# An FFT convolution with a routed expert layer behind it: where the expert work of the last pairs and the sums for their routing stand

## The chip, the core and the metric

The kernel runs on one core of one Trainium2 chip. The metric is device time in microseconds (us) for one execution. The engines are TensorE (PE; PEld is its weight loads), VectorE (DVE), ScalarE (ACT), GpSimd (POOL), and SyncE (SP), which issues most of the transfers.

## The reference

```python
Yf = rfft(x, 2 * S, axis=1) * rfft(h, 2 * S, axis=0)[None]    # x: 8 x 6336 x 128
x = irfft(Yf, 2 * S, axis=1)[:, :S]                            # a causal long convolution
scores = einsum('bsd,d->bs', x, w_gate)
out = x.copy()
for b in range(8):
    top = argpartition(-scores[b], 128)[:128]                  # 128 rows of each batch
    y = maximum(x[b, top] @ w1, 0) @ w2                        # 128 -> 1024 -> 128
    out[b, top] = x[b, top] + sigmoid(scores[b, top])[:, None] * y
```

## The kernel before

The convolution is a product of transforms over a factored length, 99 by 64. The work comes in eight **units**: a unit is a pair of batches with half of the features, so units 2p and 2p+1 make up pair p. One unit goes through four steps. `stage_a` multiplies the folded input (VectorE folds it, `fold`) by a 99-point table. `stage_b` does the 64-point transforms ("n2 visits", 13 chunks of k) and multiplies by the filter's spectrum on VectorE and GpSimd (`times`). `stage_c` goes back over 64 (64 columns s), and `stage_d` back over 99, and writes the unit out.

Before the loop, groups 0 to 15 of `stage_a` run for the filter and unit 0 (here called the start), with `fill`, a few products that nobody reads, behind every second group; then `stage_b_first`. The loop over i (**stage** i) has 32 items. Items 0 to 15 run `stage_c` of unit i, four columns each, and items 16 to 31 run `stage_d`. A `plan` puts `stage_a` of unit i+1 at items 0 to 8 and `stage_b` of unit i+1 at items 14 to 28, two chunks at a time. All instruction streams are fixed when the program is written; each engine runs its own in order.

The scores need no pass of their own: `weigh(i, c)` adds one column of the spectrum, times its gate weight, into `acc` on VectorE, 64 times per unit. These sums are emitted inside `stage_c`, ahead of column s those with n below 2s+5 in the last stage. After the sums of both units of a pair, `route(p)` goes on in small **visits**, called by `aside`: `scores`, then `pick`, an eight-way search in 11 steps (`search`: compare and count on VectorE, a small product on TensorE at line 428), then ranks, and the row numbers `iu`. Then `gather` fetches the 128 chosen rows by an indirect transfer from GpSimd's queue, for either half u of the features, and `feed` runs `expert` for both batches in visits: a transposition (line 534), two halves of the first product (line 546), and the second product (line 558), whose result goes back by two indirect transfers (line 562).

What is emitted when is set by counters that the program keeps, not by the chip: `t["pe"]` grows by 0.47 per column of `stage_c`, 0.89 per product group of `stage_d` and by the `on_pe` of the others; `t["dve"]` runs ahead of it by the `on_dve` of VectorE's work. A visit names the counter value at which the next may come (`after_dve` returns `t["dve"]` plus 0.3), and `aside` compares.

Pair 0's experts run in stage 3, pair 1's in stage 5, pair 2's in stage 7, the last one, and pair 3's behind it. What waits behind the last stage, until the last rows are written and gathered, is filled with unread products (`idle`): 9 from `route` and 5 from the closing loop.

Of the kernel before, what the change touches and what calls it, by code (L numbers as in the profile page):

```python
# [35 lines left out]
def conv_moe(ctx, tc, x, h, wg_d, w1, w2, fa_d, wb_d, wc_d, at_d, wgl_d, tri_d, cst_d, tw_d, fb_d, *out):  # L36
# [62 lines left out]
    ones16 = cp.tile([128, 128], BF16, name="ones16")  # L99
    upper16 = cp.tile([128, 128], BF16, name="upper16")  # L100
# [20 lines left out]
    def make_constants():  # L121
        v.tensor_copy(out=upper16, in_=upper)
# [180 lines left out]

    def stage_c(i):
# [90 lines left out]
    def pick(b0, ss, picked):  # L395
# [64 lines left out]
        for t in range(2):  # L460
            pe.matmul(pt[0:N1, 264 + 2 * t:266 + 2 * t], upper16[0:N1, 0:N1], rows[:, t], start=True, stop=t == 0)
        pe.matmul(pt[0:N1, 266:268], ones16[0:N1, 0:N1], rows[:, 0], start=False, stop=True)
# [23 lines left out]
        for b in range(2):  # L486
            iu = new([128, 1], U32, "iu", bufs=2)
            v.tensor_scalar(out=iu, in0=col[:, b:b + 1], scalar1=float(b0 * S), scalar2=None, op0=ALU.add)
            picked.append(iu)
# [5 lines left out]
    def gather(b0, picked, u, j, r):  # L495
        if u == 0:
            r.append((picked[j], new([CAP, 2, 64], F32, "xe", bufs=2)))
# [4 lines left out]
    def feed(b0, got, work):  # L502
        if b0 + 2 < B:
            yield after_act(16.0)
        while work is apart and phase[0] < NU - 1:
            yield 1
        todo = []
        for j, (iu, xt) in enumerate(got):
            todo.append(expert(b0, iu, xt, lambda shape, tag, j=j: work(shape, tag, j)))
# [10 lines left out]
    def shared(shape, tag, j):  # L520
        return new(shape, F32, tag)
# [8 lines left out]
    def expert(b0, iu, xt, work):  # L530
# [24 lines left out]
        yield 1  # L555
        py = ps()
        for f in range(NF):
            pe.matmul(py[:, 0:D], hm[f], w2s[:, f], start=(f == 0), stop=(f == NF - 1))  # L558
        on_pe(1.9)
# [15 lines left out]
    def route(p):  # L575
        b0 = 2 * p
        while weighed[0] < 2 * p + 2 or (fed and b0 + 2 < B):
            yield
# [4 lines left out]
        got = []  # L583
        for u in range(2):
            while (u or b0 + 2 < B) and (phase[0] < 2 * p + 2 or (b0 + 2 < B and place[0] < 4)):
                yield
            for j in range(2):
                gather(b0, picked, u, j, got)
                if b0 + 2 < B and place[0] > 10:
# [13 lines left out]
    fed = []  # L603
# [10 lines left out]
    with tc.manual_schedule():  # L614
# [16 lines left out]
        wide = acc.rearrange("p t b c k -> p (t b c k)")[:, 0:512]  # L631
        v.memset(wide[:, 128:512], 1.0)
# [5 lines left out]
        for g in range(16):  # L638
# [5 lines left out]
            if g % 2:  # L644
# [12 lines left out]
        for i in range(NU):  # L657
# [11 lines left out]
            for item in range(32):  # L669
# [13 lines left out]
                if i == NU - 1 and item == 16:  # L683
                    ready[1] = 0.0
                    aside()
                    aside()
                if item in plan:
                    aside()
                    for kind, k in plan[item]:
                        if kind == "a":  # L690
# [4 lines left out]
                            elif q == 0 and g % 8 == 7:  # L695
                                fold(g + 1, v)
# [10 lines left out]
                issue(item == 31)  # L707
            for st in (cs, ds):
# [3 lines left out]
        assert not fed  # L712
        for _ in routes:
            idle(5)
# [134 lines left out]
```

## Time and profile before

| what | value |
|---|---|
| time, median of 3 runs (lowest to highest) | 895.11 us (892.11 to 895.34) |
| the profiled execution: its time, its span | 894.62 us, 892.9 us |
| mean granted TensorE clock in it | 0.995 |
| busy: PE, DVE, ACT, POOL | 866.3, 697.3, 348.0, 304.0 us |
| the chain that ended last: PE, DVE, DMA | 77%, 14%, 4% |

The span runs from the first to the last instruction; 1.7 us of the execution lie outside it. A busy PE is not a PE at its peak, since matmuls overlap and their ends are modelled.

### The profile page before, as it was taken

What the parts mean: (1) busy time and instruction counts of PE and PEld (TensorE: products, weight loads), DVE (VectorE), ACT (ScalarE), POOL (GpSimd) and SP (SyncE); (2) the same over time, 40 slices, a digit from 0 to 9 for tenths busy, and PEclk for the clock granted to TensorE, in tenths of its full rate; (3) what the DMA queues carried; (4) which work ended last, traced back from release to release, by engine and by line L of the source; (5) the groups of instructions that cost most, each with busy time, mean ns of one, the idle gap of its engine ahead of it and who ended that gap; (6) DMA issues with size and microseconds to landing.
All of it is one profiled execution on the core that took longest, in us unless ns stands there. A gap on an engine that the chain in (4) does not pass through costs nothing.

```text
span 892.9 us, 37277 instructions
## 1 busy us (share of the span) xinstructions
PE 866.3 (97%) x16656; PEld 764.3 (86%) x16656; DVE 697.3 (78%) x1608; ACT 348.0 (39%) x405; POOL 304.0 (34%) x268
## 2 busy tenths in 40 slices
PE   8899999999999999999999999999999999999996
PEld 6699898789987998889987898889987899789875
DVE  6468976568699989967499989867589987977761
ACT  4523671147311751156401671147311572125321
POOL 0058306520355006630355105640265204650102
PEclk9999999999999999999999999999999999999998
DMA  8659567846585667655376566855467535840150
GB/s 296 208 178 356 178 217 228 265 156 193 180 279 191 199 198 244 216 191 198 107 230 208 179 209 204 262 162 178 133 216 234 183 118 157 276 140 33 33 185 28
DMA packets 76379, 170.76 MB, mean 191 GB/s; under 512 B 9786, under 2 KB 26136, under 8 KB 76219
## 3 DMA queue, kind: packets, MB, share of 16 engines
q1 hardware_dynamic: 75194, 167.32, 58.4%
q8 instruction: 131, 2.15, 1.0%
q0 software_dynamic: 1024, 1.05, 0.5%
q14 instruction: 30, 0.24, 0.1%
HBM read 135.38 MB, written 32.96 MB: 189 GB/s over the span
## 4 chain that ended last, share of the span: by engine, by line
PE 77%; DVE 14%; DMA 4%; issue 3%; ACT 1%; POOL 1%; POOLq 0%; ACTq 0%; SPq 0%; DVEq 0%
PE pb L318 26%; PE pb L348 18%; PE pb L177 12%; PE pb L214 10%; PE pb L264 4%; DVE tx L223 3%; DMA ht<-hd 3%; DVE slots L223 3%; DVE cmp L419 2%; PE m L546 1%; PE m L629 1%; PE m L558 1%; PE m L377 1%; DVE num L422 1%; DVE thr L435 1%
## 5 line engine op out<-in xcount | busy, mean ns | idle before, releaser
L234 POOL TENSOR_TENSOR slots<-slots,tx 128x512 f32<-128x512 f32 (+1 forms) x182 | 232.6, 1310 | 355.7 <-DVE tx L223 342.7
L318 PE MATMUL pb<-wc,slots 64*99 64x128 f32 x4096 | 241.5, 272 | 0.9 <-POOL slots L279 0.9
L318 PEld LDWEIGHTS pb<-wc,slots 64*99 64x99 f32 x4096 | 226.8, 167 | 9.4 <-POOL slots L279 1.3
L348 PE MATMUL pb<-slots,at 99*99 99x256 f32 (+1 forms) x1040 | 231.0, 374 | 2.5 <-issue 1.1
L348 PEld LDWEIGHTS pb<-slots,at 99*99 99x99 f32 x1040 | 161.8, 163 | 58.2 <-issue 6.0
L322 ACT COPY slots<-pb 99x1024 f32<-99x1024 f32 x128 | 143.3, 1119 | 127.2 <-PE pb L318 119.7
L359 ACT COPY yt<-pb 99x1024 f32<-99x1024 f32 x63 | 63.9, 1014 | 329.8 <-PE pb L348 324.8
L214 PEld LDWEIGHTS pb<-slots 128*64 128x64 f32 x5544 | 167.9, 136 | 14.5 <-issue 12.9
L214 PE MATMUL pb<-slots 128*64 128x64 f32 x5544 | 175.8, 222 | 1.4 <-issue 1.4
L302 DVE SCALAR_TENSOR_TENSOR acc<-slots,wgl,acc 128x198 f32<-128x198 f32 x496 | 170.2, 419 | 2.7 <-POOL slots L234 2.7
L223 DVE TENSOR_TENSOR slots<-pb,ht 128x512 f32<-128x512 f32 (+1 forms) x182 | 119.5, 657 | 47.6 <-PE pb L214 36.2
L186 ACT COPY slots<-pb 128x792 f32<-128x792 f32 x138 | 114.9, 918 | 23.9 <-PE pb L177 23.9
L223 DVE TENSOR_TENSOR tx<-pb,ht 128x512 f32<-128x512 f32 (+1 forms) x182 | 118.9, 653 | 0.0
L177 PE MATMUL pb<-fa,xr 50*64 50x99 f32 x1952 | 94.4, 248 | 1.3 <-DVE tx L276 0.9
L177 PEld LDWEIGHTS pb<-fa,xr 50*64 50x64 f32 x1952 | 85.7, 133 | 10.4 <-issue 4.9
L177 PE MATMUL pb<-fa,two 50*64 50x99 f32 x1344 | 66.0, 247 | 0.2 <-issue 0.2
L562 POOL DMA_INDIRECT out<-xe,iu x16 | 16.1, 1003 | 138.7 <-DVE xe L560 123.4
L279 POOL TENSOR_TENSOR slots<-slots,tx 128x256 f32<-128x256 f32 (+1 forms) x50 | 39.4, 809 | 58.6 <-DVE tx L276 57.3
L177 PEld LDWEIGHTS pb<-fa,two 50*64 50x64 f32 x1344 | 58.8, 132 | 0.4 <-issue 0.3
L177 PE MATMUL pb<-fa,slots 50*64 50x99 f32 x1312 | 48.9, 253 | 5.5 <-issue 5.4
L177 PEld LDWEIGHTS pb<-fa,slots 50*64 50x64 f32 x1312 | 44.4, 138 | 8.8 <-issue 6.3
L166 DVE TENSOR_TENSOR xr<-xr 128x512 f32<-128x512 f32 x61 | 42.9, 703 | 2.0
(143 smaller groups left out, 596.5 us busy)
## 6 DMA issues: line engine op xcount, KB each, us to landing
slots<-tab_wb SPq DMA_DIRECT2D x86, 512.0 KB
xr<-in_x SPq DMA_DIRECT2D x61, 512.0 KB
out<-yt SPq DMA_DIRECT2D x63, 396.0 KB
ht<-hd SPq DMA_DIRECT2D x84, 256.0 KB
at<-tab_at SPq DMA_DIRECT2D x128, 153.1 KB
hd<-slots SPq DMA_DIRECT2D x12, 512.0 KB
xr<-tab_wb SPq DMA_DIRECT2D x9, 512.0 KB
slots<-in_h SPq DMA_DIRECT2D x8, 512.0 KB
```

Source lines behind the costliest of these rows:

```text
L166: eng.tensor_tensor(out=a[:, 0], in0=a[:, 0], in1=a[:, 1], op=ALU.add)
L177: pe.matmul(pt[c * 64:c * 64 + 64, b, d * N1:(d + 1) * N1], src, fa[rows, c], start=True, stop=True)
L186: act.copy(out=dst, in_=src)
L214: pe.matmul(banks[c][g * 64:g * 64 + 64, j * 64:j * 64 + 64], wt[:, j, c * 64:c * 64 + 64], y[:, g, :, k0 + j], start=True, stop=True)
L223: v.tensor_tensor(out=dst, in0=banks[c][:, 0:kn * 64].rearrange("p (k b j t) -> p k b j t", k=kn, b=2, t=2), in1=ht[t].rearrange("p k (j t ...
L234: pool.tensor_tensor(out=d3, in0=d3, in1=tx.rearrange("p k (j t) -> p k j t", t=2), op=ALU.add if c else ALU.subtract)
L279: pool.tensor_tensor(out=d3, in0=d3, in1=tx[:, c, 0:w].rearrange("p k (j t) -> p k j t", t=2), op=ALU.add if c else ALU.subtract)
L302: v.scalar_tensor_tensor(out=dst, in0=col, scalar=w, in1=dst, op0=ALU.mult, op1=ALU.add)
L318: pe.matmul(pair[0:N1, g, s % 4 * 128:s % 4 * 128 + 128], y[rows, s // 2, ri, :, s % 2], wc[rows, ri], start=(ri == 0), stop=(ri == 1))
L322: act.copy(out=z[:, s // 4], in_=pair[0:N1].rearrange("p g (j t m) -> p (g j) t m", j=2, t=2))
L348: pe.matmul(pt[0:N1, o:o + w * 128], ats[tau // 2][:, tau % 2, c], z[:, c, q:q + w], start=(c == 0), stop=(c == 1))
L359: act.copy(out=yt.rearrange("p n b q d -> p n q b d"), in_=src.rearrange("p (n q b d) -> p n q b d", n=w, q=4, b=2))
```

## The change

It does eight things. (1) In the start, `fill` comes after groups 1 and 3 alone, with 384 columns for 512. (2) In stage 6 the n2 visits of unit 7 stand at items 11 to 23 in place of 14 to 28. (3) 30 of unit 7's 64 sums are emitted at items 26 to 31 of stage 6. (4) The first two folds of the next unit go from items 6 to 8 of a stage to items 29 and 30. (5) `feed` is no longer called from `aside` but from `feeder`, at plan items; it takes both experts of a pair one step further per visit, at least 2.5 apart. If it begins by item 8 (`alone`), the two output tiles `yt` are its scratch space, and the next `route` may begin meanwhile. (6) Of pair 2's eight expert visits three stay in the last stage and five come behind it. (7) All four gathers of pair 3 come behind the last stage, batch by batch; then pair 2's five visits, 8 unread products, the closing loop's 5, and pair 3's experts in another order. (8) The last two output tiles lie in `flat` and not in the two `yt` buffers. The diff, without some declarations:

```diff
@@ stage_c
             while n < min(64, (5 if i < NU - 1 else 8) * s // 4 + 5):
-                weigh(i, n)
+                if n >= early[0]:
+                    weigh(i, n)
                 n += 1
...
-            if i == NU - 1 or (fed and s % 4 == 1):
+            if i == NU - 1:
                 aside()
@@ stage_d
-                yt = tp.tile([N1, 2, 2, 4, 64], F32, tag="y", name="yt", bufs=2)[:, 0:w]
+                if alone:
+                    yt = flat[0:N1, 8192 + n * 512:8704 + n * 512]
+                else:
+                    yt = tp.tile([128, 1024], F32, tag="y", name="yt", bufs=2)[0:N1]
@@ feed
-        if b0 + 2 < B:
-            yield after_act(16.0)
-        while work is apart and phase[0] < NU - 1:
+        last = b0 + 4 >= B
+        if not last:
+            alone[0] = place[0] <= 8
+            if alone[0]:
+                sides = [tp.tile([128, 1024], F32, tag="y", name="yt", bufs=2) for _ in got]
+            else:
+                sides = [None, two.rearrange("p a n -> p (a n)")]
+        while last and phase[0] < NU - 1:
             yield 1
...
         if b0 + 2 == B:
-            for j in (0, 1, 0, 0, 1, 0, 1, 1, 0, 1):
-                next(todo[j], None)
+            for j in (0, 0, 0, 1, 0, 1, 1, 1):
+                next(todo[j])
+        elif last:
+            for j in (0, 1):
+                next(todo[j])
+            yield after_act(2.5)
+            while place[0] < 16:
+                yield 1
+            next(todo[0])
+            while phase[0] < NU:
+                yield 1
+            for n, j in enumerate((0, 1, 1, 0, 1)):
+                while n == 3 and not gathered[0]:
+                    yield 1
+                next(todo[j])
+                yield 1
         else:
-            for g in todo:
-                for n, _ in enumerate(g):
-                    yield after_act(1.7)
-                    while work is apart and g is todo[1] and n == 2 and place[0] < 16:
-                        yield 1
+            for _ in range(4):
+                for g in todo:
+                    next(g)
+                yield after_act(2.5)
@@ route
-        while weighed[0] < 2 * p + 2 or (fed and b0 + 2 < B):
+        while weighed[0] < 2 * p + 2 or (fed and b0 + 2 < B and not alone[0]):
             yield
...
+        if b0 + 2 == B:
+            while phase[0] < NU:
+                yield
+            for j in range(2):
+                for u in range(2):
+                    gather(b0, picked, u, j, got)
+            gathered[0] = True
+            while fed:
+                ready[1] = 0.0
+                feeder()
+            idle(8)
+            yield 0
+            yield from feed(b0, got)
+            return
...
-        if b0 + 2 < B:
-            fed.append(feed(b0, got, shared if b0 + 4 < B else apart))
-        else:
-            idle(9)
-            yield 0
-            yield from feed(b0, got, apart)
+        ready[1] = after_act(16.0)
+        fed.append(feed(b0, got))
@@ aside, which no longer feeds
-        if t["pe"] >= ready[0] and (place[0] >= 16 or phase[0] >= NU - 1 or t["dve"] < t["pe"] + 1.0):
+        if t["pe"] >= ready[0] and (quiet[0] or place[0] >= 16 or phase[0] >= NU - 1 or t["dve"] < t["pe"] + 1.0):
             ready[0] = next(routes, None) or 0.0
+
+    def feeder():
         if fed and t["pe"] >= ready[1]:
             ready[1] = next(fed[0], None) or 0.0
...
@@ the start
-                pe.matmul(pt, plain[:, 0:128], wide, start=True, stop=True)
+                pe.matmul(pt[:, 0:384], plain, wide, start=True, stop=True)
...
-            if g % 2:
+            if g in (1, 3):
                 fill(1)
@@ the loop over the stages
-                for n, at_item in enumerate((14, 16, 18, 20, 23, 26, 28)):
+                for n, at_item in enumerate((14, 16, 18, 20, 23, 26, 28) if i < NU - 2 else (11, 13, 15, 17, 19, 21, 23)):
...
-                if i == NU - 1 and item == 16:
-                    ready[1] = 0.0
-                    aside()
+                if i == NU - 1 and item <= 16:
+                    feeder()
                     aside()
                 if item in plan:
+                    if item <= 8 or alone[0] or item > 12:
+                        feeder()
                     aside()
...
-                            elif q == 0 and g % 8 == 7:
-                                fold(g + 1, v)
...
-                            if q and g % 8 == 7:
-                                fold(g + 2, v)
-                                on_dve(2.8)
...
+                if i == NU - 2 and item > 25:
+                    for _ in range(5):
+                        weigh(i + 1, early[0])
+                        early[0] += 1
+                if item in (29, 30) and i < NU - 2:
+                    fold(g0 + item - 21, v)
+                    on_dve(1.4)
...
         for _ in routes:
-            idle(5)
+            if fed and not gathered[0]:
+                ready[1] = 0.0
+                feeder()
+                idle(3)
+            else:
+                idle(5)
```

## Rows read from the trace of the kernel before

**Rows 1.** Page: engines; DMA queue (packets, MB, share); one group (count, busy, mean ns).

```profile
PE 866.3 (97%) x16656; PEld 764.3 (86%) x16656; DVE 697.3 (78%) x1608; ACT 348.0 (39%) x405; POOL 304.0 (34%) x268
...
q8 instruction: 131, 2.15, 1.0%
...
L223 DVE TENSOR_TENSOR slots<-pb,ht 128x512 f32<-128x512 f32 (+1 forms) x182 | 119.5, 657 | 47.6 <-PE pb L214 36.2
```

**Rows 2.** Busy time by stretch: span, engines (instructions), granted clock, DMA share, GB/s.

```profile
702.26:798.94 96.68, 95.40 (x1965) 84.93 (x1964) 83.16 (x189) 38.63 (x40) 37.04 (x30) 1.00 0.57 181
798.94:842.00 43.06, 43.06 (x613) 40.10 (x613) 32.53 (x106) 21.94 (x29) 2.27 (x3) 1.00 0.11 34
sum 743.55, PE 734.14 PEld 653.03 DVE 607.03 ACT 296.02 POOL 255.03; mean PE 91.77 PEld 81.63 DVE 75.88 ACT 37.00 POOL 31.88
```

**Rows 3.** Chain that ended last, the start: start us, us, what.

```profile
3.63 3.71 PE m L629 x4
...
14.30 2.52 issue
...
27.16 0.92 issue
...
28.48 1.05 PE m L629 x2
...
36.17 0.13 issue
...
40.47 0.94 issue
...
45.58 0.67 issue
...
46.98 1.06 PE m L629 x2
```

**Rows 4.** Busy time by stretch, the start, columns as in Rows 2.

```profile
18.00:20.00 2.00, 2.00 (x45) 1.75 (x48) 1.63 (x6) 0.09 (x1) 0.00 (x0) 0.50 1.04 355
...
26.00:28.00 2.00, 1.16 (x53) 1.05 (x46) 1.93 (x4) 1.79 (x3) 0.00 (x0) 1.00 0.86 239
```

**Rows 5.** Instructions in order of time, VectorE, end of the start.

```profile
47.02 0.98 DVE L183 COPY slots<-pb 128x792 f32<-128x792 f32 x1 [1.41 <-PE pb L177]
```

**Rows 6.** Chain that ended last, pair 0's experts in stage 3.

```profile
409.45 1.09 PE m L546 x8
...
418.62 1.98 PE m L558 x16
```

**Rows 7.** Instructions in order of time, VectorE, beginning of stage 7.

```profile
795.76 21.57 DVE L302 SCALAR_TENSOR_TENSOR acc<-slots,wgl,acc 128x198 f32<-128x198 f32 x64 [2.72 <-POOL slots L234]
```

**Rows 8.** Instructions in order of time, all engines, the end.

```profile
868.80 0.98 POOL L498 DMA_INDIRECT xe<-out,iu  x1 [24.84 <-DVE iu L488]
...
870.28 6.21 PE L571 MATMUL pb<-wc 128*128 128x256 f32 x28
870.73 0.59 ACT L359 COPY yt<-m 99x512 f32<-99x512 f32 x1 [1.71 <-DMA out<-yt]
874.49 0.95 POOL L498 DMA_INDIRECT xe<-out,iu  x1 [3.44 <-issue]
875.74 0.95 POOL L498 DMA_INDIRECT xe<-out,iu  x1 [0.30 <-issue]
...
877.05 0.30 PE L534 MATMUL pb<-tri,xe 128*128 128x128 f32 x1 [0.56 <-DMA xe<-out,iu]
...
885.82 0.35 DVE L560 SCALAR_TENSOR_TENSOR xe<-pb,slots,xe 128x128 f32<-128x128 f32 x1 [0.65 <-PE pb L558]
```

**Rows 9.** Chain that ended last, the last pair's experts.

```profile
878.63 2.68 PE pb L546 x24
881.31 1.79 PE pb L558 x16
```

**Rows 10.** Line 562, the writing back of expert rows: issue to landing.

```profile
DMA to landing us min/median/max: 2.1/2.2/6.9
```

More of the change, by code (lines that the diff above doesn't have):

```diff
@@ L98, in conv_moe @@
     fb = cp.tile([N1, 2, N1], F32, name="fb")
-    ones16 = cp.tile([128, 128], BF16, name="ones16")
-    upper16 = cp.tile([128, 128], BF16, name="upper16")
+    ones16 = cp.tile([N1, N1], BF16, name="ones16")
+    upper16 = cp.tile([N1, N1], BF16, name="upper16")
     block16 = cp.tile([128, 128], BF16, name="block16")
@@ L121, in make_constants @@
     def make_constants():
-        v.tensor_copy(out=upper16, in_=upper)
+        v.tensor_copy(out=upper16, in_=upper[0:N1, 0:N1])
         v.tensor_tensor(out=within16[:, 0:128], in0=upper, in1=ident, op=ALU.add)
@@ L302, in weigh @@
             v.scalar_tensor_tensor(out=dst, in0=col, scalar=w, in1=dst, op0=ALU.mult, op1=ALU.add)
+    early = [0]
     def stage_c(i):
@@ L460, in pick @@
         for t in range(2):
-            pe.matmul(pt[0:N1, 264 + 2 * t:266 + 2 * t], upper16[0:N1, 0:N1], rows[:, t], start=True, stop=t == 0)
-        pe.matmul(pt[0:N1, 266:268], ones16[0:N1, 0:N1], rows[:, 0], start=False, stop=True)
+            pe.matmul(pt[0:N1, 264 + 2 * t:266 + 2 * t], upper16, rows[:, t], start=True, stop=t == 0)
+        pe.matmul(pt[0:N1, 266:268], ones16, rows[:, 0], start=False, stop=True)
         first = new([N1, 4], F32, "first")
@@ L486, in pick @@
         for b in range(2):
-            iu = new([128, 1], U32, "iu", bufs=2)
+            iu = new([128, 1], U32, "iu", bufs=4)
             v.tensor_scalar(out=iu, in0=col[:, b:b + 1], scalar1=float(b0 * S), scalar2=None, op0=ALU.add)
@@ L496, in gather @@
         if u == 0:
-            r.append((picked[j], new([CAP, 2, 64], F32, "xe", bufs=2)))
+            if b0 + 2 < B:
+                xe = new([CAP, 2, 64], F32, "xe", bufs=2)
+            else:
+                xe = flat[:, 14336 + j * 128:14464 + j * 128].rearrange("p (u d) -> p u d", u=2)
+            r.append((picked[j], xe))
         pool.indirect_dma_start(
@@ L500, in gather, with feed @@
             in_offset=bass.IndirectOffsetOnAxis(ap=picked[j][:, 0:1], axis=0))
-    def feed(b0, got, work):
-        if b0 + 2 < B:
-            yield after_act(16.0)
-        while work is apart and phase[0] < NU - 1:
+    def feed(b0, got):
+        last = b0 + 4 >= B
[6 more added lines that the diff above has]
+        while last and phase[0] < NU - 1:
             yield 1
@@ L508, in feed, with shared, beside @@
         for j, (iu, xt) in enumerate(got):
-            todo.append(expert(b0, iu, xt, lambda shape, tag, j=j: work(shape, tag, j)))
-        if b0 + 2 == B:
-            for j in (0, 1, 0, 0, 1, 0, 1, 1, 0, 1):
-                next(todo[j], None)
-        else:
-            for g in todo:
-                for n, _ in enumerate(g):
-                    yield after_act(1.7)
-                    while work is apart and g is todo[1] and n == 2 and place[0] < 16:
-                        yield 1
-    def shared(shape, tag, j):
-        return new(shape, F32, tag)
+            if last:
+                work = lambda shape, tag, j=j: apart(shape, tag, (b0, j))
+            elif sides[j] is None:
+                work = shared
+            else:
+                work = lambda shape, tag, j=j: beside(sides[j], j, shape, tag)
+            todo.append(expert(b0, iu, xt, work))
+        if b0 + 2 == B:
+            for j in (0, 0, 0, 1, 0, 1, 1, 1):
[14 more added lines that the diff above has]
+                yield 1
+        else:
+            for _ in range(4):
+                for g in todo:
+                    next(g)
+                yield after_act(2.5)
+    def shared(shape, tag):
+        return new(shape, F32, tag + "0" if tag in ("xet", "gg") else tag)
+    alone = [False]
+    def beside(side, j, shape, tag):
+        if tag in ("xet", "gg"):
+            return new(shape, F32, tag + str(j))
+        n = ("half", "hf", "m", "cmp", "hit").index(tag) % 4 * 256
+        r = side[0:shape[0], n:n + shape[1] * (shape[2] if len(shape) > 2 else 1)]
+        return r.rearrange("p (a b) -> p a b", b=shape[2]) if len(shape) > 2 else r
     spare = {}
@@ L555, in expert @@
         yield 1
+        on_pe(1.9)
         py = ps()
@@ L558, in expert @@
             pe.matmul(py[:, 0:D], hm[f], w2s[:, f], start=(f == 0), stop=(f == NF - 1))
-        on_pe(1.9)
         v.scalar_tensor_tensor(out=xe, in0=py[:, 0:D], scalar=gg[:, 0:1], in1=xe, op0=ALU.mult, op1=ALU.add)
@@ L583, in route @@
         got = []
+        if b0 + 2 == B:
[12 more added lines that the diff above has]
+            return
+        quiet[0] = True
         for u in range(2):
-            while (u or b0 + 2 < B) and (phase[0] < 2 * p + 2 or (b0 + 2 < B and place[0] < 4)):
+            while phase[0] < b0 + 2 or place[0] < 4:
                 yield
@@ L588, in route @@
                 gather(b0, picked, u, j, got)
-                if b0 + 2 < B and place[0] > 10:
+                if place[0] > 10:
                     yield after_act(2.0)
-        if b0 + 2 < B:
-            fed.append(feed(b0, got, shared if b0 + 4 < B else apart))
-        else:
-            idle(9)
-            yield 0
-            yield from feed(b0, got, apart)
+        quiet[0] = False
+        ready[1] = after_act(16.0)
+        fed.append(feed(b0, got))
     def all_routes():
@@ L602, in conv_moe @@
     ready = [0.0, 0.0]
-    fed = []
+    fed, quiet, gathered = [], [False], [False]
     routes = all_routes()
     def aside():
-        if t["pe"] >= ready[0] and (place[0] >= 16 or phase[0] >= NU - 1 or t["dve"] < t["pe"] + 1.0):
+        if t["pe"] >= ready[0] and (quiet[0] or place[0] >= 16 or phase[0] >= NU - 1 or t["dve"] < t["pe"] + 1.0):
             ready[0] = next(routes, None) or 0.0
+    def feeder():
         if fed and t["pe"] >= ready[1]:
@@ L628, in fill @@
             for _ in range(n):
-                pe.matmul(pt, plain[:, 0:128], wide, start=True, stop=True)
-        wide = acc.rearrange("p t b c k -> p (t b c k)")[:, 0:512]
-        v.memset(wide[:, 128:512], 1.0)
+                pe.matmul(pt[:, 0:384], plain, wide, start=True, stop=True)
+        wide = acc.rearrange("p t b c k -> p (t b c k)")[:, 0:384]
+        v.memset(wide[:, 128:384], 1.0)
         fill(2)
@@ L711, in conv_moe @@
         phase[0] = NU
-        assert not fed
         for _ in routes:
-            idle(5)
+            if fed and not gathered[0]:
+                ready[1] = 0.0
+                feeder()
+                idle(3)
+            else:
+                idle(5)
 def _order():
```

1 line of the change is left out of this document (added).

## Prediction

> **What bounds the kernel now.** I read the busy times by stretch first, one stretch for each of the stages 0 to 6. Over these and the first 43.06 us of stage 7, TensorE is busy 734.14 of 743.55 us [rows 2], so all its waiting there comes to 9.41 us. VectorE has more room: in stage 6 it is busy 83.16 of 96.68 us. In stages 0 to 7 only less TensorE work makes the kernel shorter by much; a wait removed from another engine can give back at most those 9.4 us. Two other places remain. In the start, the chain shows TensorE stopping with nothing it waits for ("issue"), 2.52, 0.92, 0.94 and 0.67 us long [rows 3]. At the end, the instructions in order of time show TensorE on unread products for 6.21 us from 870.28 on, then waiting until 877.05, when the first gathered rows of pair 3 are there [rows 8].
>
> My sum stands against the profiled execution's 894.62 us, of which the trace covers 892.9; the median of the runs shown, 895.11, is 0.5 us higher.
>
> **The start.** The first fill, four products of 512 columns, takes 3.71 us, each later one (two products) 1.05 [rows 3]. At 384 columns the first costs 2.78, so the first input group can start 0.93 sooner; the fill behind group 1 gives 0.26. Six fills fall away, 6 x 1.05 = 6.3 us of TensorE. How much of that is on the path depends on the gaps. The page counts 131 instruction transfers of 2.15 MB, 16.4 KB each, against 2 x 16,656 TensorE instructions, so about 254 instructions to a transfer [rows 1]. Two groups of `stage_a` and a fill are 130 products by the code, with as many weight loads: 260. The gaps come once for each two groups, at 36.17, 40.47 and 45.58, 4.3 and 5.1 us apart. I read them as TensorE having used up one block of instructions before the next is there. Then a block lasts as long as its transfer, however little work is in it, and a fill in a block that ends in a gap costs nothing. That holds for the removed fills of the blocks with the gaps at 27.16, 40.47 and 45.58; that of the block ending at 36.17, gap 0.13, can hardly be shortened either. The last fill, 46.98 to 48.04, lies beside VectorE's copy from 47.02 to 48.00 [rows 5], on which the next step waits anyway. The one at 28.48 lies in a block with no gap and could give 0 to 1.05; I take 0.3. The sum is 0.93 + 0.26 + 0.3 = **1.5 us** less; bounds are 0, and 0.93 + 0.52 + 6.3 = 7.7.
>
> The Trainium skill (Runtime: NRT & Kernel Launch, section Instruction fetch mechanics) also has blocks of 256 instructions, the next one fetched while the current one runs, but says that crossing into the next is mostly hidden. By that the fills would count in full. The gaps in [rows 3] speak against it here.
>
> **Stages 0 to 6.** The experts of pairs 0 and 1 keep their work: a visit of half a first product took 1.09 us and one of the second 1.98 [rows 6]. Whether both experts come in one visit or in two leaves the products on TensorE the same. Two visits, at items 14 and 16, now stand beside the n2 chunks: GpSimd's four write-backs, 0.95 and a gap of 0.30 each by its gathers [rows 8], 5 us in all, queue ahead of `times`' additions, and VectorE's sigmoid steps ahead of its multiplications. The scores' products follow at item 16 and give them time. The folds keep their cost and come where VectorE has room. I take 0 for all of it. It can gain at most the 9.4 us of TensorE's waits, of which I allow 2, and lose about as much.
>
> Stage 6 gets 30 of the 64 sums; 64 took 21.57 us, 0.337 each [rows 7], so 10.1 us more for VectorE. Its idle 13.5 us [rows 2] cover that with 3.4 left. The sums read all of unit 7's columns, so they wait for GpSimd's last addition; VectorE waited 2.72 us for it before the first sum [rows 7]. With the chunks ending at item 23, that addition is done before item 26. What cannot run in time runs in stage 7, where VectorE is idle 43.06 - 32.53 = 10.5 us of the stretch in rows 2. Queued behind late sums is the rest of pair 2's search, which nothing needs before stage 7. Cost 0; without that cover, up to 5 us.
>
> **Stage 7.** TensorE has no wait in it (43.06 of 43.06 [rows 2]), so work removed shortens it. Five visits leave: three halves and two second products, 3 x 1.09 + 2 x 1.98 = **7.2 us** less. The routing must still end within the stage. By the program's counters, the 64 sums put `t["dve"]` at 21.8 before, and the scores came at 22.7. Now 34 sums begin at column 13 (6.1): 17.8, scores at 18.3. Following the visits: the search's products come after columns 51, 57 and 63, then in `stage_d`, which has 33 product groups, at groups 2, 5, 8, 12, 15, 18, 21 and 24, the ranks at 26 and 27, the last product of `pick` at 31. Two groups, about 1.8 us, remain for the row numbers, so the pick ends with the stage.
>
> **Behind it.** Before, the stage ended near 870.1; pair 3's experts began 6.95 us later, took 8.8 until 885.82, and 7.1 more ran to the end of the span [rows 8]: 22.8. Now TensorE first has pair 2's five visits at the rates without interruption, 2.68 for three halves and 1.79 for a second product [rows 9]: 6.3 us. Behind them, in order, stand 8 + 5 unread products, 13 x 6.21 / 14 = 5.8 us. So pair 3 begins 12.0 us after the stage. The gathers are no longer the limit: the third began 4.4 us after the stage, held by the last writes; the last output copy had waited 1.71 us for its buffer [rows 8], past the stage's end by some 0.4. From 4.0 on come three gathers 1.25 apart, the last at 6.5, landing 2.5 later (874.49 to 877.05), at 9.0. With all rows there, pair 3's work is 0.6 for transpositions, 0.4 for a copy, 3.6 and 3.6: 8.1. Sum: 12.0 + 8.1 + 7.1 = 27.2, or 4.4 more than before.
>
> **Sum.** -1.5 (start) + 0 - 7.2 (stage 7) + 4.4 (behind it) = -4.3: 894.6 - 4.3 = **890.3 us**.
>
> **Rivals.** *The fills were on the path.* The gaps would close when less is issued, because the transfers had been running ahead. The stretch from 28.1 to 36.2 with only one gap of 0.13 speaks for it; gaps at nearly every block elsewhere speak against. Then the start gives up to 7.7 in place of 1.5; with 6.5 the time is 885.3. *The end gives everything back.* Pair 2's write-backs write the output that pair 3's gathers read, so they begin at 9.0 and end at 9.0 + 4 x 1.25 = 14; if one takes 6.9 us to land, as the slowest did [rows 10], pair 3's first write-back, due about 17.5, waits until 21, and the last ends 2.6 later. That leaves a total of -1.7, 892.9 us. *The clock falls.* After the gap at 14.30 the granted clock was 0.50 between 18 and 20, and stayed at 1.00 with TensorE 58% busy between 26 and 28 [rows 4]. Without fills the gaps grow; a block at half clock costs about 1.5 us more, but fits in the 5 us of its transfer, and only the first products behind the start pay: 1.7 us. The total is then -2.6, 892.0 us. The Trainium skill (TensorE: Matmul & The Clock Gate, section on the HAM clock gate) says that the throttled state is the default and activity releases it; the 0.50 in rows 4 agrees. *Slower.* In stage 6 the n2 chunks at items 11 to 15 meet the rest of unit 6's sums, the search and their own table loads. VectorE has 3.4 us left there. If its work comes in the wrong order, TensorE waits for the three PSUM buffers. A chunk that misses them costs its four multiplications, 4 x 0.657 = 2.6 us [rows 1]; four such chunks, 10.5 us, give +6.2, 900.8 us. It decides from two chunks on.
>
> **How the numbers follow.** Forecast as summed, 0.50 (888 to 892.3); fills on the path, 0.20; the end gives it back, 0.17; the clock, 0.06; slower, 0.07. A measurement of this kernel can tell about 0.5%, 4.5 us, from no change. The forecast lies at that border: of its half I put 0.30 beyond it and 0.20 within. Faster: 0.30 + 0.20 = 0.50; same: 0.20 + 0.17 + 0.06 = 0.43; slower: 0.07. The range leaves out the slower case and the far ends of the others: 885 to 894.5.
>
> **What would show it.** In the start, gaps of about 2 us after each two groups, as far apart as before, show the block reading right; groups 2.9 us apart show it wrong. Stage 7 should last about 64 us to its last product, with the last gather's instruction some 6.5 us behind. Unread products that end well after the last gather has landed would show the term of 4.4 right; pair 3 waiting for rows would show it wrong. TensorE's waits in stage 6 should stay near 1.3 us. The prediction fails if the fills count in full, if stage 6 grows, or if the pick ends after the stage.

## The result and the profile after

The changed kernel takes 884.66 us (median of 5 runs, 882.97 to 885.49) against 895.11 us (5 runs, 892.11 to 897.31): ratio 0.9884, 95% interval 0.986 to 0.9908. Three further comparisons of the same two kernels, on three chips, gave 0.9922 [0.9894, 0.9949], 0.991 [0.9877, 0.9944] and 0.99 [0.9867, 0.9934]. So the change is worth 7 to 10 us. The forecast was 4.3, and 884.66 lies 0.3 us below the range.

The profiled execution has a span of 882.6 us, 10.3 less than before. I cut both spans at the first product of `stage_c` (or of the next stage's work) of each stage and at the last product of `stage_d`; the start ends where `stage_c` runs on without a break, 1.0 us behind its first four products:

| stretch | before, us | after, us | difference | forecast |
|---|---|---|---|---|
| start, to the unbroken run of `stage_c` | 98.45 | 97.34 | -1.1 | -1.5 |
| stages 0, 1, 2, 4 together | 385.85 | 383.48 | -2.4 | 0 |
| stages 3 and 5 together (experts of pairs 0, 1) | 217.96 | 212.44 | -5.5 | 0 |
| stage 6 | 96.68 | 98.88 | +2.2 | 0 |
| stage 7, to its last product | 71.5 | 63.65 | -7.9 | -7.2 |
| behind it | 22.4 | 26.8 | +4.4 | +4.4 |

The three terms that were worked out come out within 0.7 us, the start's by luck, as the experiments show. What fails is the zero for stages 0 to 6. On the page, TensorE has 14 instructions fewer than in [rows 1], but 10.8 us less busy time, and as many instruction transfers:

```profile
PE 855.5 (97%) x16642; PEld 764.3 (87%) x16642; DVE 699.1 (79%) x1608; ACT 348.0 (39%) x405; POOL 323.3 (37%) x268
...
q8 instruction: 131, 2.15, 1.0%
```

Busy times by stretch, columns as in [rows 2]: the second 18 to 20 us as in [rows 4], then stages 3, 6 and 7.

```profile
18.00:20.00 2.00, 1.76 (x3) 0.50 (x2) 0.73 (x4) 0.87 (x1) 0.00 (x0) 0.50 0.90 327
383.94:490.51 106.57, 105.45 (x2044) 94.18 (x2047) 86.60 (x191) 41.95 (x52) 37.53 (x30) 1.00 0.61 190
693.26:792.14 98.88, 96.25 (x1964) 85.17 (x1964) 90.93 (x212) 38.87 (x40) 41.56 (x29) 1.00 0.57 176
792.14:855.79 63.65, 62.93 (x697) 53.83 (x697) 45.61 (x145) 27.45 (x29) 14.44 (x3) 1.00 0.32 97
```

In stage 6 TensorE's idle time is 2.63 us where it was 1.28 [rows 2]; in stage 3 TensorE itself is busy 2.1 us less than before (107.54). The chain in the start, the rows that answer to [rows 3], shows the same kind of gaps, and the weights' step beginning at 47.05, before at 48.03. Its first lines show the first input group waiting for the filter's rows:

```profile
1.21 4.53 DMA slots<-in_h
...
7.24 4.80 PE pb L177 x126
...
15.78 2.46 issue
...
28.03 1.95 issue
...
40.68 1.31 issue
...
44.96 0.48 issue
...
47.05 2.99 PE pb L264 x48
```

The end, in order of time, answers to [rows 8]: the third gather's instruction at 861.90, the unread products until 867.83, the gate of pair 3's first expert on VectorE, which needs its rows, at 863.04, and its transposition on TensorE only at 867.66.

```profile
861.90 0.95 POOL L509 DMA_INDIRECT slots<-out,iu  x1 [0.30 <-issue]
862.05 5.78 PE L615 MATMUL pb<-wc 128*128 128x256 f32 x26
...
863.04 0.29 DVE L582 TENSOR_TENSOR slots<-slots,wg 128x128 f32<-128x128 f32 x1 [0.44 <-DMA slots<-out,iu]
...
867.66 0.27 PE L578 MATMUL pb<-tri,slots 128*128 128x128 f32 x1
...
872.29 0.35 DVE L604 SCALAR_TENSOR_TENSOR slots<-pb,slots 128x128 f32<-128x128 f32 x1 [0.24 <-PE pb L603]
872.91 0.97 POOL L606 DMA_INDIRECT out<-slots,iu  x1 [2.59 <-DVE slots L604]
```

### The profile page after: what moved, and what is told of

It reads as the page before. It is cut to its first block, busy times and chain, and to the rows that moved or that the text cites. A ratio compares the mean times of both kernels' runs of the same rounds, so it can differ in the third digit from the quotient of the medians.

```text
span 882.6 us, 37258 instructions
## 1 busy us (share of the span) xinstructions
PE 855.5 (97%) x16642; PEld 764.3 (87%) x16642; DVE 699.1 (79%) x1608; ACT 348.0 (39%) x405; POOL 323.3 (37%) x268
## 4 chain that ended last, share of the span: by engine, by line
PE 76%; DVE 15%; DMA 3%; issue 3%; ACT 1%; POOL 1%; POOLq 0%; SPq 0%; DVEq 0%; ACTq 0%
PE pb L321 26%; PE pb L351 18%; PE pb L177 13%; PE pb L214 10%; DVE tx L223 4%; PE pb L264 4%; DVE slots L223 4%; DMA ht<-hd 3%; DVE cmp L426 3%; PE m L603 1%; PE m L590 1%; DVE thr L442 1%; PE m L384 1%; DVE num L429 1%; PE pb L615 1%
## 5 line engine op out<-in xcount | busy, mean ns | idle before, releaser
L321 PE MATMUL pb<-wc,slots 64*99 64x128 f32 x4096 | 236.6, 271 | 0.9 <-POOL slots L279 0.9
L177 PE MATMUL pb<-fa,slots 50*64 50x99 f32 x1312 | 52.0, 268 | 6.9 <-issue 6.2
L177 PEld LDWEIGHTS pb<-fa,slots 50*64 50x64 f32 x1312 | 48.2, 150 | 8.4 <-issue 4.8
L429 DVE TENSOR_REDUCE num<-cmp 128x7 bf16<-128x693 bf16 x44 | 38.6, 878 | 1.5
```

The costliest lines, as they stand in the source:

```text
L177: pe.matmul(pt[c * 64:c * 64 + 64, b, d * N1:(d + 1) * N1], src, fa[rows, c], start=True, stop=True)
L429: v.tensor_reduce(out=num, in_=cmp, axis=AX.X, op=ALU.add)
```

## The experiments

Every kernel's time stands beside runs of the kernel before on the same chip; those medians lay between 893.98 and 895.25 us, single runs between 889 and 904, so a kernel's median is good to about 1 us, and stage lengths and rows by line tell more than the times.

**What the edits of stages 0 to 5 do.** The kernel after again, and with one edit undone in each, on one chip: the fills, the folds, and the visits with both experts (one expert per visit again, inside `stage_c`).

```diff
 e1   pt[:, 0:384] -> pt, and fill(1) behind every odd group
 e2  -if item in (29, 30) and i < NU - 2: fold(g0 + item - 21, v)
     +folds beside the eighth group, as before
 e3  -for _ in range(4):
     -    for g in todo: next(g)
     +for g in todo:
     +    for _ in range(4): next(g); yield after_act(1.7)
     +stage_c: elif s % 4 == 1: feeder()
```

> The changed kernel once more, as the reference for the three others on the same chip and to see which gaps of its trace come back. If the shorter stages 0, 1, 3 and 5 are its own, the stage lengths repeat within 0.5 us: 91.7, 98.8, 96.1, 106.6, 96.9, 105.9, 98.9. If stage 0's gain of 1.7 us was one lost wait of 1.37 us that comes and goes, stage 0 is either 91.7 or 93.3.

> The changed kernel with the eight fills of 512 columns of before. Theory (a block of instructions lasts as long as its transfer): the start is 1.0 to 1.5 us longer and the kernel 1 to 1.5 us slower. Rival (the fills were on the path, and the start's gaps are something else): about 6 us slower. A third reading, that the fills' instructions shift the blocks and with them the gap of 1.37 us in stage 0: stage 0 goes back from 91.7 to 93.3.

> The changed kernel with the next unit's first two folds at items 6 to 8 again. Theory (the folds at items 29 and 30 spare TensorE waits at each stage's beginning): stages 1 to 5 0.5 to 1 us longer each, the kernel 2 to 4 us slower. Rival (the folds are free at either place): within 1 us.

> The changed kernel with pairs 0 and 1 served as before: one expert after the other, visits 1.7 apart, also between the columns of stage_c; scratch space as in the changed kernel. Theory (each visit costs a break in stage_c's products, eight breaks against four, and the short ones cost more): stages 3 and 5 go from 106.6 and 105.9 to 108.5 to 109.5, the kernel 5 us slower. Rival (the visits are free in either form, the stages got shorter for another reason): within 1 us.

Measured: again 0.9922; fills back 0.9951 [0.9925, 0.9977]; folds back 0.9945 [0.9927, 0.9964]; one expert per visit 0.9935 [0.9912, 0.9958]. The intervals overlap, so the times don't tell these four apart; the losses of 1 to 5 us that the theories named came out in the medians as 2.0, 2.9 and 0.9 us against after again. The traces say more. With all fills back the weights' step begins at 46.72 us, without them at 46.66: where 1.0 to 1.5 us were expected, the fills cost nothing. With the folds back stages 0 to 6 sum to 698.1 us, without to 699.3: nothing there, against the theory. Its stage 7, though, lasts 65.4 us in place of 63.7, with TensorE waiting 1.5 us for pair 2's rows; that is one execution. With one expert per visit stages 3 and 5 last 109.23 and 108.50 us, against 108.06 and 107.42, and before 109.44 and 108.52. After again itself does not repeat the first profile's 106.6 and 105.9 within the 0.5 us expected.

**The kernel before again**, with three experiments on the end and on stage 6. Without its `yield`, e6 loses the closing loop's 5 unread products too, so all 13.

```diff
 e4  -... else (11, 13, 15, 17, 19, 21, 23)       n2 visits at 14 to 28
     -if i == NU - 2 and item > 25: ... weigh     no early sums
 e5   all eight visits of pair 2 inside stage 7
 e6  -idle(8)
     -yield 0
```

> The kernel before, unchanged, to see how far its stages repeat. First theory (the visits with both experts of a pair shorten the stages with experts): stages 0 to 5 of this execution last together about 603 us again, as in the first profile of before (603.8) and in the kernel after with one expert per visit (603.2), and not the 600.0 of the kernel after run again; stages 3 and 5 lie at 108.5 to 109.5. Rival (chance gaps): the sum of stages 0 to 5 lies anywhere between 598 and 604, and the 1.4 us gap in stage 0 is gone. Ratio to before 1.000 +- 0.003 by both.

> The kernel after, with the seven n2 visits of stage 6 at their old items and none of the 30 early sums. First theory: stage 6 loses its 1.5 to 2.2 us (98.2 to 98.9 -> about 96.7), stage 7 has all 64 sums on VectorE again, its pick ends about 3 us later, behind the last product, and the gathers start 1 to 4 us later: tail 27 -> 28 to 31, whole time within +-2 us of the kernel after. Rival (the sums in stage 6 cost nothing, another cause makes it longer): stage 6 stays at 98 to 99 and the time rises by 1 to 4 us.

> The kernel after, with all eight visits of pair 2 back inside stage 7. First theory: stage 7 takes back its 7.5 us (63.7 -> 71), the tail loses the four it gained (26.8 -> 22.8), so the time rises by about 3.5 us against the kernel after in the same call. Rival (the scatters and their landing set the end, not the products): the tail stays at 25 or more and the time rises by 6 to 7 us. Second rival (stages 0 to 6 make all of the gain): within 1 us of the kernel after.

> The kernel after without the 13 idle products between pair 2's and pair 3's experts. First theory (TensorE's queue sets the end): pair 3's transpose starts when its rows are there, about 4.6 us sooner (863 instead of 867.7), and the tail falls from 26.8 to 22.2 to 23.5, the lower end only if GpSimd's queue, which scatters pair 2's rows until 869 + 1.3, lets it: time 3.3 to 4.6 us lower. Rival (the clock): in the gap of about 1 us TensorE is granted the low clock, the 24 + 32 products behind it (6 us) take twice as long, and the time is 1 to 2 us higher. Stages 0 to 5 are the kernel after's: by the theory of the visits they sum to 599 to 601.

| kernel | ratio to before | stage 3 | stage 5 | stage 6 | stage 7 | behind it |
|---|---|---|---|---|---|---|
| before again | 0.9996 [0.9973, 1.002] | 109.83 | 108.82 | 96.39 | 71.6 | 22.2 |
| e4 | 0.991 [0.9875, 0.9944] | 106.39 | 105.80 | 96.84 | 63.5 | 28.9 |
| e5 | 0.9941 [0.9916, 0.9965] | 105.87 | 105.81 | 98.34 | 70.7 | 22.1 |
| e6 | 0.9885 [0.9847, 0.9923] | 106.39 | 105.89 | 97.64 | 63.65 | 23.3 |

Before repeats its stages 3 and 5 (218.65 us together, 217.96 in the first profile). The three kernels with the visits of after have 211.7 to 212.3, the four executions of after itself 212.4, 215.5, 214.3 and 212.2, all below before: that gain is no chance, but its size varies with gaps that come and go. But before's stage 0, 93.35 us with a gap of 1.4, is 91.98 here: a good part of the 2.4 us in the other stages is chance. In e4 stage 6 has its old length again, and the end is 2.1 us longer than after's. e5 shows the trade of stage 7 for the end: 7.0 us back in the one, 4.7 off the other, net 2.4 us worse. e6 shows that the unread products were most of the +4.4: pair 3's transposition comes at 859.68, as soon as pair 2's products are done, 6.5 us behind the stage instead of 11.9, and 3.5 us come off the end of this execution. The rival that the clock falls in the wait did not happen: there is almost no wait, as e6's chain shows.

```profile
855.97 3.62 PE m L603 x32
859.59 0.09 issue
859.68 0.31 PE pb L578
```

**Why stages 3 and 5 are shorter.** The chain of e0, stage 3, then that of the kernel after in a fourth run, the same stretch:

```profile
406.60 1.06 PE pb L318 x16
407.65 1.09 PE m L546 x8
408.74 1.93 PE pb L318 x32
...
416.82 1.98 PE m L558 x16
...
430.94 2.80 PE pb L318 x48
```

```profile
404.11 3.68 PE pb L321 x64
407.79 1.98 PE m L590 x16
...
423.32 1.98 PE m L590 x16
...
432.90 3.77 PE m L603 x32
```

Sixteen, 32, 48 and 64 products of `stage_c` take 1.06, 1.93, 2.80 and 3.68 us: 0.87 for each sixteen, and 0.19 once per run. Eight products of the experts take 1.09, 16 take 1.98: 0.89 for eight, and 0.20 once. A visit in the middle of `stage_c` thus pays twice, for itself and for the second half of the run that it cuts. Before, eight visits in each of stages 3 and 5 made eight cuts; after, four visits stand where one kind of work ends and another begins, and cut none. 8 runs of `stage_c` and 4 of experts less, by estimate 12 x 0.19 = 2.3 us for each stage.

Behind products of their own shape the experts pay nothing of it: 16 took 1.79 us behind the first products [rows 9], and 32 took 3.62 above, against 1.98 and 3.77 between runs of `stage_c`. The Trainium skill (TensorEngine Tiling (Array Packing), section Key Properties) states it as a rule: a change of tiling mode drains TensorE. `stage_c` contracts over 64 rows, the experts over 128; the runs agree, at 0.15 to 0.20 us a change. Products of 128 rows are not needed for it: ahead of `stage_a`, whose products contract over 50 rows (line 177, `50*64` in the rows by line, `64*99` for `stage_c`), 64 products of `stage_c` take as long. The first profile of after, end of the start:

```profile
103.08 3.67 PE pb L321 x64
106.76 2.21 PE pb L177 x88
```

Two kernels were made to test it; in each the lines that start the visits moved, and nothing else:

```diff
 e8 (after)   +elif s % 4 == 1 and phase[0] < NU - 1: feeder()     in stage_c
              -if item <= 8 or alone[0] or item > 12: feeder()
 e9 (before)  -if i == NU - 1 or (fed and s % 4 == 1):             in stage_c
              +if i == NU - 1:
```

> The kernel after once more, for a comparison on one chip. Theory (each run of like products on TensorE has a fixed price of about 0.19 us: the chain of before shows 16, 32, 48, 64 stage-c products in 1.06, 1.93, 2.80, 3.67 us): stage-c products of stage 3 take 29.5 us as in the other two executions, against 31.5 in the kernel before, whatever else varies. Rival (chance gaps): they lie between 29.5 and 31.5. Ratio to before 0.988 to 0.993.

> The kernel after with its visits of pairs 0 and 1, both experts together as before, put inside runs of stage-c products (behind the second of four) and not between runs. Theory of the runs: four runs of stage c are cut in two in each of stages 3 and 5, 4 x 0.19 = 0.8 us more on TensorE in each, stage-c products 29.5 -> 30.2 us, expert products as in the kernel after (8.1 to 8.3 us); stages 3 and 5 together 1.5 us longer. Rival (that both experts come together is what saves): the two stages last as in the kernel after, within 0.5 us.

> The kernel before, its visits of one expert each put between runs of stage c and the other stages' work and not inside runs of stage c; three of them now cut runs of stage b in two. Theory of the runs: eight cuts of stage-c runs fall away in each of stages 3 and 5 (-1.5 us; stage-c products 31.5 -> about 30), three cuts of stage-b runs come (+0.6): 0.9 us less in each, about -1.8 in all, ratio 0.998, which the times alone can hardly tell; the rows by line can. Rival (the number of visits, not their place, counts): stage-c products stay at 31.5 us and both stages last 109 +- 0.7 as in the kernel before.

The groups of `stage_c`'s products in stage 3 (operation, shapes, count; busy us, mean ns; idle before): e0, e3, e8, e9 and the third run of after, in this order.

```profile
L318 PE MATMUL pb<-wc,slots 64*99 64x128 f32 x512 | 31.5, 274 | 0.0
```

```profile
L321 PE MATMUL pb<-wc,slots 64*99 64x128 f32 x512 | 31.5, 274 | 0.0
```

```profile
L321 PE MATMUL pb<-wc,slots 64*99 64x128 f32 x512 | 30.5, 272 | 0.0
```

```profile
L318 PE MATMUL pb<-wc,slots 64*99 64x128 f32 x512 | 29.5, 271 | 0.0
```

```profile
L321 PE MATMUL pb<-wc,slots 64*99 64x128 f32 x512 | 29.5, 271 | 0.0
L214 PE MATMUL pb<-slots 128*64 128x64 f32 x792 | 25.6, 222 | 0.8 <-issue 0.8
```

Eight cuts 31.5, four cuts 30.5 (30.7 in stage 5), none 29.5 (29.5 to 29.8 over all executions): 0.25 us a cut. It is the place that counts, in e9 with one expert per visit as well. The lengths are less clean. After's third run has in stages 3 and 5 a gap of 0.8 us within the n2 products (last row), which e8 has not; so e8 is shorter in all, 106.77 and 106.97 against 107.10 and 107.15, where 0.8 us more each was expected; TensorE's busy time is 0.4 and 0.6 us longer in e8. e9 wins 3.5 us in stage 3 against e0, and no time in all: ratio 1.000 [0.998, 1.002]. Its stage 5 has "issue" gaps of 1.9 us and 6.3 us less VectorE work (81.69 us; before 88.02), and stage 6 is 1.6 to 1.9 us longer than before's, so work of stage 5 has moved there. Some of it is pair 2's search: of its eleven products (line 428) before has six in stage 5 and five in stage 6, e9 four and seven. Pair 1's has moved by one in the same way, out of stage 3, so not all of the 3.5 us is the price of cuts.

**Why stage 6 is longer**, and how much of the end can be had.

```diff
 e10 -idle(8)
     -yield 0
     -for j in range(2): for u in range(2): gather(b0, picked, u, j, got)
     +for u in range(2): for j in range(2): gather(b0, picked, u, j, got)
 e11  n2 visits at 14 to 28, early sums kept
 e12  n2 visits early, no early sums
 e13  e10 with e11's n2 visits
 e14  e10, n2 visits at 14, 16, 18, 20, 22, 24, 26
 e15  e10, n2 visits at 13, 15, 17, 19, 21, 23, 25
```

> The kernel after without the 13 idle products, and with pair 3's four gathers by halves of a row (both experts' first halves, then both second halves), so that one gather more is done while the last output is being written. Theory (behind the last product GpSimd's queue is the limit once the idle products are gone): the last gather ends 1.25 us sooner (859.7 -> 858.4), the scatters follow, and the tail falls from 23.3 without the idles alone to 22.0 to 22.6; against the kernel after in the same call 4 to 5 us less, ratio to before 0.984 to 0.988. Rival (TensorE's 19 us of products behind the stage are the limit): the tail stays at 23.3 +- 0.3.

> The kernel after with stage 6's n2 visits at their old items and the 30 early sums kept. If the early n2 visits make stage 6 longer: stage 6 falls from the 97.9 to 98.9 of the four executions of the kernel after to 96.5 to 97, and stage 7 and the tail keep 63.7 and 26.8. If the early sums do, by their 20 us of VectorE: stage 6 stays at 97.9 or more, since the last n2 chunks now come where the sums stand.

> The kernel after without the 30 early sums, the n2 visits early as in it. If the sums make stage 6 longer: stage 6 falls to 96.5 to 97; if the n2 visits do, it stays at 97.9 or more. Both expect the pick of the last pair later, as in the kernel with both undone, and a tail of 28.5 to 30 in place of 26.8: time 0 to 2 us above the kernel after.

> The best version by the runs so far: the kernel after without the 13 idle products, pair 3's gathers by halves, stage 6's n2 visits at their old items, sums early. Tail 22.4 as without the idles with the gathers by halves, stage 7 63.7; stage 6 about 97 if the early n2 visits are what makes it longer, 98 or more otherwise. Ratio to before 0.984 to 0.988.

> The kernel after, for a comparison with the next two on one chip: ratio to before 0.988 to 0.993, stage 6 97.9 to 98.9, tail 26.8.

> The kernel after without the 13 idle products, gathers by halves, and stage 6's n2 visits at items 14 to 26 in place of 11 to 23, so that all of them still stand ahead of the first early sum. If the place of the visits inside stage c is what costs in stage 6, it takes 96.5 to 97 and the time is 6 us below the kernel after (4.4 in the tail, 1.7 in stage 6). Rival (the hurry before the sums costs, wherever the visits begin): stage 6 stays at 98 or more, and 4.4 us are won.

> As the kernel with the visits at items 14 to 26, with them one item sooner, 13 to 25: one chunk pair begins inside stage c. Stage 6 between that kernel's and 97.9; 5 to 6 us below the kernel after.

| kernel | median, us | ratio to before | stage 6 | stage 7 | behind it |
|---|---|---|---|---|---|
| after, third and fourth run | 885.75, 884.86 | 0.991, 0.99 | 97.91, 97.75 | 63.65 | 26.8 |
| e10 | 884.26 | 0.9874 [0.9849, 0.9899] | 97.99 | 63.65 | 22.4 |
| e11 | 883.06 | 0.9863 [0.9822, 0.9905] | 96.53 | 63.65 | 26.7 |
| e12 | 887.52 | 0.989 [0.985, 0.9931] | 98.28 | 63.5 | 30.4 |
| e13 | 879.02 | 0.9812 [0.9772, 0.9852] | 96.42 | 63.65 | 22.2 |
| e14 | 882.92 | 0.9879 [0.9829, 0.9929] | 96.95 | 67.7 | 22.1 |
| e15 | 881.32 | 0.9843 [0.9798, 0.9887] | 97.94 | 64.9 | 21.8 |

In e11 and e13 the ten sums at items 26 and 27 are taken before the last n2 chunk, at item 28, has written its part of the columns, so ten of 64 terms are partly of old values; the instructions are the same. They show that the early n2 visits make stage 6 longer, not the sums: without the sums (e12) it keeps 98.28. TensorE's groups in stage 6, after and e11:

```profile
L351 PE MATMUL pb<-slots,at 99*99 99x256 f32 (+1 forms) x132 | 29.5, 374 | 1.7 <-ACT slots L325 1.2 <-DVE tx L223 0.5
```

```profile
L351 PE MATMUL pb<-slots,at 99*99 99x256 f32 (+1 forms) x132 | 29.3, 374 | 0.0
```

The first n2 chunks stand inside `stage_c`, and the first product of `stage_d` then waits 1.2 us for the copy of the last `stage_c` tile, a later one 0.5 for VectorE; the cuts add 0.6 us of `stage_c` (30.4; 29.8 in e11). What the early sums buy is seen in the end, 26.8 us with them and 30.4 without (e12). VectorE's sums of unit 7 (line 302) and pair 3's row numbers (line 495), in after, e12 and e11 (there the last 54 of the 64):

```profile
782.76 21.56 DVE L302 SCALAR_TENSOR_TENSOR acc<-slots,wgl,acc 128x198 f32<-128x198 f32 x64
854.21 0.23 DVE L495 TENSOR_SCALAR iu<-col 128x1 uint32<-128x1 f32 x2
```

```profile
778.82 21.55 DVE L302 SCALAR_TENSOR_TENSOR acc<-slots,wgl,acc 128x198 f32<-128x198 f32 x64
854.39 0.23 DVE L495 TENSOR_SCALAR iu<-col 128x1 uint32<-128x1 f32 x2
```

```profile
790.24 18.21 DVE L302 SCALAR_TENSOR_TENSOR acc<-slots,wgl,acc 128x198 f32<-128x198 f32 x54 [0.88 <-POOL slots L234]
853.53 0.23 DVE L495 TENSOR_SCALAR iu<-col 128x1 uint32<-128x1 f32 x2
```

In after and in e12 the sums run at the same time, from 9.4 us ahead of stage 7 to 12.2 us into it, whether they are emitted early or not. Yet the row numbers are there 1.35 us ahead of the stage's end in after (855.79) and 2.96 us behind it in e12 (851.66). In e11 the sums end 4.8 us later in the stage than in after, and the row numbers stand at 1.35 us again. So it is not the time at which VectorE does the sums that counts. The code offers the reason: each sum adds 0.34 to `t["dve"]`, and with 30 fewer of them in stage 7 the scores and the search are emitted sooner. The early n2 visits are needed only so that the columns are complete when the sums at items 26 and 27 read them. That is worth 3.6 us at the end for the 1.1 to 2.5 us that stage 6 pays. Sums from item 28 on, with the n2 visits at their old items, were not tried. e14 and e15 try other items for the visits. With the visits at 14 to 26 stage 6 has its old length and stage 7 loses 4 us, 2.1 of them in TensorE waiting for pair 2's rows; one item sooner, stage 6 is as long as after's and stage 7 loses 1.2, 1.0 of it in such a wait. Neither beats after's items in these stages. e10 itself has the 4.4 us less behind the stage, but only 1.5 in the median: stages 0 to 6 of its profiled execution were 2.5 us longer than in after's third run. e14 and e15 have 4.7 and 5.0 us less behind the stage: their medians are 1.9 and 3.5 us below that of after on the same chip, where 6 and 5 to 6 were expected, and the intervals overlap with after's.

## Why the prediction was too small

**The start: the reading of the gaps holds, the 1.5 us do not.** Gaps of 0.3 to 2.5 us stay with the fills gone, and six fills put back move the start by 0.06 us. The traces' transfers bear the block reading out: in before every gap of the start ends 1.2 to 1.5 us behind the end of an instruction transfer, in the four executions of after 1.1 to 1.5. The Trainium skill (Runtime: NRT & Kernel Launch, section Instruction fetch mechanics) calls the crossing mostly hidden; here it isn't, and the runs decide. But e1 undoes the term of 1.5 whole and moves the start by 0.06. Its largest part, 0.93 for the first fill, was taken for granted: the first group begins at 7.24, before at 7.34 [rows 3], because it then waits for the filter's rows and VectorE's work on them. That -1.1 lies near -1.5 is luck: in four executions of after `stage_c`'s unbroken run began at 96.05 to 98.74 us, in two of before at 98.45 and 98.17. The 885.3 us of the rival with the fills on the path is near the measured time, for another reason.

**Stages 0 to 6: the step that failed** is "Whether both experts come in one visit or in two leaves the products on TensorE the same", and the 0 taken from it. The products are the same; what they take is not. TensorE is busy 2.1 us less in stage 3 and 2.6 in stage 5 (105.08; before 107.68), which added to the forecast makes -4.3 - 4.7 = -9.0; that still counts the start's 1.5, which no run shows. The bound in the same paragraph, the 9.4 us of TensorE's waits, bounded the wrong thing: the gain came out of its busy time. The price stood in the rows: a visit of 16 second products took 1.98 us in [rows 6] and 1.79 in [rows 9], and I used that difference for the end without asking what it was.

**Stage 6: its 0 was mis-sized** by +1.1 to +2.5 us (97.75 to 98.88 in four executions of after, 96.68 and 96.39 in two of before). The mechanism feared, n2 chunks that meet a full VectorE, is there with 0.5 us, beside 1.2 for a copy. The 10.1 us of sums cost nothing, as forecast, but for another reason than VectorE's room: the edit does not change when they run (e12). The rival of 900.8 us didn't come about.

**Stage 7: right in kind**, -7.9 for -7.2. Visits no longer cut `stage_c` there either: its products take 29.5 us, before 31.0; 0.5 us goes back into a wait for ScalarE's copy near the stage's end.

**Behind it: right**, +4.4. Pair 3 begins 11.9 us behind the stage (forecast 12.0) and waits for the unread products, not for rows: its gate was computed 4.6 us before. The rival in which the write-backs give the gain back did not come about; pair 3's first write-back left 0.3 us after its sum.

**The clock: it fell for longer, and cost nothing that can be seen.** 18 to 20 us shows 0.50 (1.2 of 2.4 GHz) as before. But after's granted clock was low for longer, TensorE having stood still for 2.46 us (to 18.24) and 1.95 us (to 29.98) before. Busy times by stretch, after, then before:

```profile
21.00:24.00 3.00, 3.00 (x81) 3.00 (x80) 2.91 (x7) 1.79 (x2) 0.00 (x0) 0.50 0.85 279
32.00:34.00 2.00, 2.00 (x56) 1.96 (x49) 1.18 (x2) 1.78 (x3) 0.00 (x0) 0.50 0.57 127
```

```profile
21.00:24.00 3.00, 2.67 (x71) 1.90 (x66) 1.62 (x5) 2.33 (x3) 0.00 (x0) 0.97 0.89 329
32.00:34.00 2.00, 2.00 (x50) 1.12 (x46) 0.52 (x1) 1.68 (x3) 0.00 (x0) 1.00 0.86 248
```

By the clock records of the traces the start of after has 10 to 14 us at 0.50 in its four executions, that of before 3.4 and 6.9, and e1, with the fills back, 3.4. So the rival's first step happened. Its price of 1.7 us didn't: after again, with 10 us at the low clock, and e1 reach the weights' step at 46.66 and 46.72; no run separates the clock's share from that of the fills.

So 0 - 4.7 + 1.1 to 2.5 - 7.9 + 4.4 gives -5.7 to -7.1 us that the edits explain; four comparisons gave 7 to 10. The rest of the first profile, 1.1 us in the start and 2.4 us in stages 0, 1, 2 and 4, is not explained by an edit: these stages sum to 383.1 to 384.6 us in four executions of after, and to 384.2 and 385.9 in two of before.

## What to carry to other kernels

Count where a kind of product begins, not only how many there are: a small piece of work with another shape costs its own start and that of the run it cuts, so it goes where the kind changes anyway. A bound from idle time holds only for gains out of waits; ask also what makes the busy engine's instructions longer. Products that nobody reads, placed to bridge a wait, have to be weighed again when real work takes their place: here they held back the last pair by 5.4 us (11.9 against 6.5 behind the stage). And when an edit moves work in a program of fixed streams, the trace has to show whether the work itself runs at another time, or only what is emitted behind it.

## What was not expected of the hardware

Between products of different shapes TensorE loses about 0.19 us per run (1.06, 1.93, 2.80, 3.68 us for 16 to 64 products of `stage_c`), whether the neighbour contracts over 128 rows or over 50, and none is to be seen between products of one shape (the experts' 16 in 1.79 us).

In 20 executions every gap of over 0.1 us in the start that waits for nothing the profile shows ends 1.1 to 1.6 us behind the end of a 16 KB instruction transfer, and so does before's gap of 1.37 us in stage 0 (1.35 us behind). The 0.8 us within the n2 products of stages 3 and 5 are something else: two gaps of 0.4 us, 0.7 to 0.8 us apart, which end anywhere from 0.1 to 9 us behind such a transfer. They stood in after's second and third runs, on two chips, and in neither the first nor the fourth; on the chip of the third, e10 has them and e8 has none. What brings them in one execution and not in the next stays open.
